# First block of linear attention: loads in longer runs on two queues, plain float32 products, q's maxima on GpSimd

## The chip, the cores and the metric

The kernel runs on one core of one Trainium2 chip. The metric is the device time of one execution in microseconds, the median of several runs.

## The reference

Linear attention over 8 batches, 8 heads, 576 positions and 64 columns, then two feed-forward layers on the 4608 resulting rows of 512:

```python
q_s = exp(q - max(q, axis=-1)); q_s = q_s / (sum(q_s, axis=-1) + 1e-9)
k_s = exp(k - max(k, axis=2));  k_s = k_s / (sum(k_s, axis=2) + 1e-9)
kv  = einsum('bhsd,bhse->bhde', k_s, v)
x   = einsum('bhsd,bhde->bhse', q_s, kv)      # then heads side by side: 4608 x 512
r   = maximum(x @ w_in, 0)                    # 512 -> 2048
x   = (r * r) @ w_out                         # 2048 -> 512
g   = x @ w_gate                              # 512 -> 1536
out = (g / (1 + exp(-g)) * (x @ w_val)) @ w_out2
```

The weights come as 64-bit floating-point numbers; the kernel turns their bits into float32 on chip.

## The kernel before

**Blocks.** The 4608 rows are worked in 9 blocks of 512. For each block the attention of four pairs of heads (hp 0 to 3) gives four tiles xT; the first layer multiplies them by 16 tiles of w_in (`h_mm`, PSUM tiles `ph`), squares the positive part (`g_of`), and multiplies by 16 tiles of w_out into four accumulators (`acc_mm`, tiles `acc`). The main loop interleaves these with the attention of the next block. The gated layer follows for all blocks and is not touched.

**Precision.** Most products are made of float32 values split in two float32r parts, hi (a copy on ScalarE, L104) and lo (the remainder, L105, on VectorE or GpSimd); `mm3` (L110) adds three products of the parts.

**The attention of a pair.** `kv_unit` takes k's maxima over the positions (L336 to L338, a transposition L341, L343, a transposition back L346), subtracts them (L347), takes Exp (L353), and multiplies by v with a column of ones beside it (L358, 12 float32 matmuls of 65 columns, in two halves of the output), so that column 64 holds the sums; L363 and L364 take the reciprocals, L367 scales into `kf`, and `split` writes the parts to `kvs`. `q_unit` takes q's maxima (L376), Exp in 8 activations with the maximum as bias (L380), sums and reciprocals (L383 to L385), and a multiplication on GpSimd (L386). `q_transpose` transposes the result (L393) and splits it; `x_pair` multiplies the parts of kv and qT and splits the product into xT.

**The start.** No work of an earlier block covers the first block. Its tiles lie in slots of the weights' pool `wpb` (`borrowed`). All loads are issued on SP, whose order is the program's (`manual_schedule`): k0 k1 q0 v0 k2 q1 k3 v1 w v2 w q2 q3 w v3, where w is the next raw weight tile. The order on the other engines is a planner's; the program gives each step a tick: `steps` holds for each pair the ticks of kv_unit, q_unit, q_transpose and x_pair, and a unit goes on by one `yield` per tick. Two steps of the weights stand in the same plan, at ticks 5 and 8.

**Weights.** `Weights.step` takes a loaded tile through `bits_of` (L138 on ScalarE, L140, L144 and L148 on VectorE, in a PSUM buffer `pa` that the attention's small products use too; there are two), then a hi copy on ScalarE (L189) and a lo remainder on GpSimd (L191), and loads a further tile. All 32 tiles of the first layer are made while block 0 runs. Later loads reuse buffers that become free when the bits of an earlier tile are done.

## Time and profile before

| | us |
|---|---|
| median of 3 runs | 1699.56 |
| lowest and highest run | 1696.88, 1700.6 |
| the profiled execution | 1697.3 |
| span of its instructions | 1695.2 |
| TensorE busy | 1664.2 (98%) |
| VectorE, ScalarE, GpSimd busy | 930.4, 865.3, 273.8 |
| chain that ended last: TensorE | 91% |

Times in the rows are microseconds from the start of the span, durations of single instructions are nanoseconds where the view says so. PE is TensorE and PEld its weight loads, DVE is VectorE, ACT ScalarE, POOL GpSimd, SP the engine that issues DMAs (SPq: its sequencer). Matmuls overlap, so their busy time is that of the union. `L105` is line 105 of the kernel before, often a helper's line.

### The profile page before, as it was taken

The numbers are of one execution on the slowest core, as the hardware profiler recorded it, in microseconds if no ns is written. First come the engines' busy times: TensorE is split into PE (matmuls) and PEld (weight loads), VectorE is DVE, ScalarE is ACT, GpSimd is POOL, SyncE is SP. The second block draws the span as 40 slices with busy tenths as digits, with TensorE's granted clock in tenths as the row PEclk, the third lists the DMA queues.
The fourth block names the chain that finished last, engine by engine and source line by source line (L and its number), as shares of the span: only waits on it lengthen the run. The fifth ranks groups of instructions, "written<-read, shape, count | busy, mean of one in ns | idle before, by whom it ended". The sixth has DMA issues, their size and how long they took to land.

```text
span 1695.2 us, 23439 instructions
## 1 busy us (share of the span) xinstructions
PE 1664.2 (98%) x8406; PEld 1377.4 (81%) x8406; DVE 930.4 (55%) x1650; ACT 865.3 (51%) x1701; POOL 273.8 (16%) x260
## 2 busy tenths in 40 slices
PE   5999999999999999999999999999999999999998
PEld 3778888878888887788788888888878888888898
DVE  7884545555554564554242457644765476446646
ACT  6885656555565655665443345333543354335434
POOL 2661101112010111111000211021101210121020
PEclk9999999999999999999999999999999999999999
DMA  9653434443443434332233677867686678666897
GB/s 231 177 165 89 128 108 134 144 115 111 128 128 120 144 124 115 108 131 88 81 100 99 191 217 215 248 196 214 212 244 192 205 214 260 197 199 203 252 387 276
DMA packets 221315, 292.00 MB, mean 172 GB/s; under 512 B 124816, under 2 KB 152464, under 8 KB 221200
## 3 DMA queue, kind: packets, MB, share of 16 engines
q1 hardware_dynamic: 220080, 289.33, 55.6%
q8 instruction: 67, 1.10, 0.3%
q10 hardware_dynamic: 1120, 1.18, 0.2%
q14 instruction: 48, 0.39, 0.1%
HBM read 238.55 MB, written 51.90 MB: 171 GB/s over the span
## 4 chain that ended last, share of the span: by engine, by line
PE 91%; DVE 3%; DMA 2%; ACT 2%; issue 1%; POOL 0%; SPq 0%; DVEq 0%; ACTq 0%; POOLq 0%
PE ps L110 45%; PE ph L110 22%; PE acc L110 21%; PE pa L358 1%; PE pa L393 1%; DMA od<-wst 1%; DMA x<-x2d 1%; DVE wst L105 1%; ACT wst L104 0%; ACT w L380 0%; DMA wraw<-in_moe_w_out_dram 0%; DVE wbits L148 0%; DMA kt<-in_k_dram 0%; DVE pa L144 0%; DVE xT L105 0%
## 5 line engine op out<-in xcount | busy, mean ns | idle before, releaser
L110 PE MATMUL ps<-xo,wu 128*128 128x512 f32 (+1 forms) x2520 | 518.2, 368 | 0.0
L110 PEld LDWEIGHTS ps<-xo,wu 128*128 128x128 f32 x2520 | 439.0, 189 | 78.7
L110 PE MATMUL acc<-g,w 128*128 128x512 f32 x1728 | 433.1, 396 | 4.6 <-ACT g L104 1.8
L110 PE MATMUL ph<-xT,w 128*128 128x512 f32 x1728 | 421.4, 393 | 2.3 <-ACT w L189 1.2
L110 PEld LDWEIGHTS ph<-xT,w 128*128 128x128 f32 x1728 | 321.8, 188 | 72.9 <-ACT w L189 1.6
L110 PEld LDWEIGHTS acc<-g,w 128*128 128x128 f32 x1728 | 316.3, 188 | 76.1 <-DVE g L105 4.1
L110 PE MATMUL ps<-uo,wu 128*128 128x512 f32 (+1 forms) x1260 | 259.9, 368 | 1.3 <-DVE uo L105 1.3
L110 PEld LDWEIGHTS ps<-uo,wu 128*128 128x128 f32 x1260 | 219.3, 189 | 41.2 <-DVE uo L105 2.1
L460 ACT ACTIVATE r<-ph 128x512 f32<-128x512 f32 x144 | 86.3, 599 | 220.6 <-PE ph L110 220.2
L105 DVE TENSOR_TENSOR g<-r,g 128x512 fp32r<-128x512 f32 x128 | 91.5, 715 | 190.4 <-ACT g L104 190.4
L104 ACT CAST uo<-u 128x512 fp32r<-128x512 f32 (+1 forms) x210 | 120.8, 580 | 124.7 <-PE ps L110 53.4
L659 POOL TENSOR_TENSOR u<-u 128x512 f32<-128x512 f32 (+1 forms) x30 | 35.4, 1181 | 761.2 <-DVE u L655 761.2
L105 DVE TENSOR_TENSOR uo<-u,uo 128x512 fp32r<-128x512 f32 (+1 forms) x210 | 131.6, 645 | 47.4 <-ACT uo L104 47.3
L654 DVE TENSOR_TENSOR u<-u,ps 128x512 f32<-128x512 f32 (+1 forms) x60 | 38.0, 634 | 215.9 <-ACT u L653 215.9
L609 ACT COPY ps<-ps 128x512 f32<-128x512 f32 x126 | 72.0, 571 | 136.6 <-PE ps L110 135.4
L461 ACT ACTIVATE r<-r 128x512 f32<-128x512 f32 x144 | 91.2, 633 | 3.0
L104 ACT CAST g<-r 128x512 fp32r<-128x512 f32 x144 | 89.4, 621 | 3.2
L235 POOL TENSOR_TENSOR wsum<-wbits 128x256 f32<-128x256 f32 x36 | 35.3, 990 | 308.4 <-DVE wbits L148 255.0
L380 ACT ACTIVATE qs<-qs,qm 128x64 f32<-128x64 f32 x256 | 69.6, 340 | 21.0 <-DVE qm L376 15.5
L386 POOL TENSOR_TENSOR qs<-qs,qr 128x512 f32<-128x512 f32 x32 | 34.4, 1076 | 250.8 <-DVE qr L385 146.5
L653 ACT ACTIVATE u<-ps 128x512 f32<-128x512 f32 (+1 forms) x60 | 33.4, 556 | 51.6 <-PE ps L110 51.5
L618 ACT COPY p<-ps 128x512 f32<-128x512 f32 x63 | 37.1, 588 | 41.6 <-PE ps L110 40.9
(111 smaller groups left out, 1404.5 us busy)
## 6 DMA issues: line engine op xcount, KB each, us to landing
wu<-gvd SPq DMA_DIRECT2D x210, 512.0 KB, 4.4
wu<-od SPq DMA_DIRECT2D x105, 512.0 KB, 4.4
gvd<-wst SPq DMA_DIRECT2D x84, 256.0 KB, 2.3
od<-wst SPq DMA_DIRECT2D x42, 256.0 KB, 2.2
w<-in_moe_w_in_dram SPq DMA_DIRECT2D x16, 512.0 KB, 6.5
w<-in_moe_w_out_dram SPq DMA_DIRECT2D x16, 512.0 KB, 5.2
x2d<-e SPq DMA_DIRECT2D x32, 256.0 KB, 2.4
x<-x2d SPq DMA_DIRECT2D x32, 256.0 KB, 5.4
```

Source lines behind the costliest of these rows:

```text
L104: nc.scalar.copy(hi, src)
L105: (eng or nc.vector).tensor_tensor(lo, src, f32(hi), op=ALU.subtract)
L110: nc.tensor.matmul(ps, lhsT=w[s], rhs=x[t], start=start and n == 0, stop=stop and n == 2, skip_group_check=more,)
L235: nc.gpsimd.tensor_tensor(to, x, y, op=op)
L380: nc.scalar.activation(t[:, j, h], t[:, j, h], AF.Exp, bias=m[:, j, h:h + 1])
L386: nc.gpsimd.tensor_tensor(t, t, r.unsqueeze(3).to_broadcast([P, TJ, 2, D]), op=ALU.mult)
L460: nc.scalar.activation(r, ph, AF.Relu)
L461: nc.scalar.activation(r, r, AF.Square)
L609: nc.scalar.copy(x, y)
L618: nc.scalar.copy(x, y)
L654: nc.vector.tensor_tensor(u, u, gate, op=ALU.mult)
L659: nc.gpsimd.tensor_tensor(s1, a21, a22, op=ALU.add)
```

## The change

- **v** lies in its tile as ones, two rows of 64 columns, ones: 130 columns for two chunks, so each transferred run is 512 B instead of 256 B. Of a pair of chunks the first is multiplied with the ones ahead of it, the second with the ones behind it, and the sums gather in columns 0 and 65 of the product. Column 65 is opened by two matmuls of one column of zeros (`zero`) for every kv_unit; L363 adds both columns.
- **q of block 0** is one DMA per pair, with runs of 1 KB, into a tile in the order (h, j); q_unit writes its result to a second tile in the order (j, h).
- **Queues**: v0 and v1 are issued on ScalarE; SP's order becomes k0 q0 k1 q1 k2 v2 q2 k3 v3 q3 w w w. ScalarE does one Exp of a single column ahead of its loads.
- **Block 0 in plain float32**: every pair has a kf of its own (`first[hp][1]`); q_transpose only copies; x_pair is one float32 matmul of 512 columns. The split of kv into `kvs`, which block 1 needs, moves to tick 10, its remainder to GpSimd.
- **q's maxima**: for pairs 1 to 3 of block 0 GpSimd adds the negative maxima to the whole tile, and ScalarE takes one Exp of 512 columns instead of 8 of 64.

```diff
--- before.py
+++ after.py
@@ -278,7 +278,8 @@
 
     kvs = [att.tile([P, NP, 2, P], F32R, name=f"kv{i}") for i in range(2)]
     kf = att.tile([P, P], F32, name="kf")
-    vt1 = att.tile([CK, 2, NC, D + 1], F32, name="vt")
+    vt1 = att.tile([CK, 2, NC // 2, 2 * D + 2], F32, name="vt")
+    zero = const.tile([P, 1], F32, name="zero")
     kts, qs, qT, xT = {}, {}, {}, {}
 
     def load_k(b, hp, t=None):
@@ -287,12 +288,22 @@
         nc.sync.dma_start(t, k[b, 2 * hp:2 * hp + 2].rearrange("h (p c) d -> p h c d", c=NC))
         return t
 
-    def load_v(b, hp, t=None):
+    def v_words(words):
+
+        t = words[:CK, 0:NC * (2 * D + 2)].rearrange("p (h m e) -> p h m e", h=2, m=NC // 2)
+        v_ones(t)
+        return t
+
+    def v_ones(t):
+        nc.gpsimd.memset(t[:, :, :, 0:2 * D + 2:2 * D + 1], 1.0)
+
+    def load_v(b, hp, t=None, by=nc.sync):
         if t is None:
             t = vt1
         for h in range(2):
-            nc.sync.dma_start(
-                t[:, h, :, 0:D], v[b, 2 * hp + h].rearrange("(p c) d -> p c d", c=NC)
+            by.dma_start(
+                t[:, h, :, 1:2 * D + 1],
+                v[b, 2 * hp + h].rearrange("(p m x) d -> p m (x d)", m=NC // 2, x=2),
             )
         return t
 
...
-    def kv_unit(b, hp):
+    def kv_unit(b, hp, kf=kf):
...
@@ -353,31 +363,51 @@
         pk = ps_a.tile([P, T], F32, name="pa", tag="pa")
+        for j in range(2):
+            nc.tensor.matmul(
+                pk[j * D:(j + 1) * D, D + 1:D + 2], lhsT=kt[:, j, 0, :], rhs=zero[:CK],
+                start=True, stop=False, skip_group_check=True,
+            )
         for c in range(NC):
+            m, x = divmod(c, 2)
             for j in range(2):
                 nc.tensor.matmul(
-                    pk[j * D:(j + 1) * D, 0:D + 1], lhsT=kt[:, j, c, :], rhs=vt[:, j, c, :],
-                    start=(c == 0), stop=(c == NC - 1),
+                    pk[j * D:(j + 1) * D, x:x + D + 1], lhsT=kt[:, j, c, :],
+                    rhs=vt[:, j, m, x * (D + 1):(x + 1) * (D + 1)],
+                    start=(c == 0), stop=(c == NC - 1), skip_group_check=True,
                 )
         rd = col.tile([P, 1], F32, name="rd", tag="rd", bufs=1)
-        nc.vector.tensor_scalar(rd, pk[:, D:D + 1], EPS, None, op0=ALU.add)
+        nc.vector.tensor_scalar(rd, pk[:, 0:1], pk[:, D + 1:D + 2], EPS, op0=ALU.add, op1=ALU.add)
         nc.vector.reciprocal(rd, rd)
         for j in range(2):
             r = slice(j * D, (j + 1) * D)
-            nc.scalar.activation(kf[r, r], pk[r, 0:D], AF.Copy, scale=rd[r])
+            nc.scalar.activation(kf[r, r], pk[r, 1:D + 1], AF.Copy, scale=rd[r])
+        if b:
+            kv_split(b, hp, kf)
+        yield
+
+    def kv_split(b, hp, kf, eng=None):
         kv = kvs[b % 2]
-        split(kv[:, hp, 0], kv[:, hp, 1], kf)
-        yield
+        split(kv[:, hp, 0], kv[:, hp, 1], kf, eng)
 
     def q_unit(i, hp):
 
         t = qs.pop((i, hp))
         m = sp.tile([P, TJ, 2], F32, name="qm", tag="qm")
-        nc.vector.tensor_reduce(m, t, axis=AX.X, op=ALU.max, negate=True)
-        yield
-        for j in range(TJ):
-            for h in range(2):
-                nc.scalar.activation(t[:, j, h], t[:, j, h], AF.Exp, bias=m[:, j, h:h + 1])
+        src = t
+        if i == 0:
+            src, t = src[0].rearrange("p h j d -> p j h d"), t[1]
+        nc.vector.tensor_reduce(m, src, axis=AX.X, op=ALU.max, negate=True)
+        yield
+        if i == 0 and hp:
+            nc.gpsimd.tensor_tensor(
+                t, src, m.unsqueeze(3).to_broadcast([P, TJ, 2, D]), op=ALU.add
+            )
+            nc.scalar.activation(t, t, AF.Exp)
+        else:
+            for j in range(TJ):
+                for h in range(2):
+                    nc.scalar.activation(t[:, j, h], src[:, j, h], AF.Exp, bias=m[:, j, h:h + 1])
         yield
         r = sp.tile([P, TJ, 2], F32, name="qr", tag="qr")
         nc.vector.tensor_reduce(r, t, axis=AX.X, op=ALU.add)
@@ -393,7 +423,9 @@
             nc.tensor.transpose(pt.rearrange("r (p j) -> r j p", j=TJ)[:, j], src[:, j], ident)
         if t is None:
             t = qtp.tile([P, 2, T], F32R, name="qT", tag="qT")
-        split(t[:, 0], t[:, 1], pt)
+            split(t[:, 0], t[:, 1], pt)
+        else:
+            nc.scalar.copy(t, pt)
         qT[i, hp] = t
 
     def x_pair(i, hp):
@@ -402,7 +434,9 @@
         else:
             px = ps_acc.tile([P, T], F32, name="acc", tag="acc")
         t = qT.pop((i, hp))
-        for p0, n, b, _ in runs(i):
+        if i == 0:
+            nc.tensor.matmul(px, lhsT=first[hp][1], rhs=t, start=True, stop=True)
+        for p0, n, b, _ in runs(i) if i else ():
             kv = kvs[b % 2]
             c = slice(p0 * TJ, (p0 + n) * TJ)
             mm3(px[:, c], (kv[:, hp, 0], kv[:, hp, 1]), (t[:, 0, c], t[:, 1, c]), True, True)
@@ -706,20 +740,32 @@
 
 
     with tc.manual_schedule(engines={mybir.EngineType.SP}):
-        nc.gpsimd.memset(vt1[:, :, :, D:D + 1], 1.0)
+        v_ones(vt1)
+        nc.gpsimd.memset(zero, 0.0)
         nc.gpsimd.memset(kf, 0.0)
 
 
         def borrowed():
             return f32(w_slot(wpb)).rearrange("p t n -> p (t n)")
 
+        first = []
         for hp in range(NP):
             kt = borrowed()[:CK, 0:2 * NC * D].rearrange("p (h c d) -> p h c d", h=2, c=NC)
-            vt = borrowed()[:CK, 0:2 * NC * (D + 1)].rearrange("p (h c d) -> p h c d", h=2, c=NC)
-            nc.gpsimd.memset(vt[:, :, :, D:D + 1], 1.0)
-            qt = borrowed()[:, 0:T].rearrange("p (j h d) -> p j h d", h=2, j=TJ)
+            vt = v_words(borrowed())
+            words = borrowed()
+            qt = (
+                words[:, 0:T].rearrange("p (h j d) -> p h j d", h=2, j=TJ),
+                words[:, T:2 * T].rearrange("p (j h d) -> p j h d", h=2, j=TJ),
+            )
             kts[0, hp], qs[0, hp] = (kt, vt), qt
-        for what in "k0 k1 q0 v0 k2 q1 k3 v1 w v2 w q2 q3 w v3".split():
+            words = borrowed()
+            first.append((words[:, 0:T], words[:, T:T + P]))
+            nc.gpsimd.memset(first[hp][1], 0.0)
+        warm = sp.tile([P, TJ, 2], F32, name="qm", tag="qm")
+        nc.scalar.activation(warm[:, 0, 0:1], zero, AF.Exp)
+        load_v(0, 0, kts[0, 0][1], nc.scalar)
+        load_v(0, 1, kts[0, 1][1], nc.scalar)
+        for what in "k0 q0 k1 q1 k2 v2 q2 k3 v3 q3 w w w".split():
             if what == "w":
                 w1.load()
                 continue
@@ -729,15 +775,19 @@
             elif what[0] == "v":
                 load_v(0, hp, kts[0, hp][1])
             else:
-                load_q(0, hp, qs[0, hp])
+                nc.sync.dma_start(
+                    qs[0, hp][0].rearrange("p h j d -> p h (j d)"),
+                    q[0, 2 * hp:2 * hp + 2, 0:T, :].rearrange("h (p j) d -> p h (j d)", j=TJ),
+                )
 
         plan = []
         steps = ((1, 1, 5, 8), (1, 2, 5, 9), (2, 3, 7, 10), (4, 4, 8, 10))
         for hp, (n_kv, n_q, n_t, n_x) in enumerate(steps):
-            plan.append((n_kv, lambda hp=hp: kv_unit(0, hp)))
+            plan.append((n_kv, lambda hp=hp: kv_unit(0, hp, first[hp][1])))
             plan.append((n_q, lambda hp=hp: q_unit(0, hp)))
-            plan.append((n_t, lambda hp=hp: q_transpose(0, hp, w_slot(wpb))))
+            plan.append((n_t, lambda hp=hp: q_transpose(0, hp, first[hp][0])))
             plan.append((n_x, lambda hp=hp: x_pair(0, hp)))
+            plan.append((10, lambda hp=hp: kv_split(0, hp, first[hp][1], nc.gpsimd)))
         plan += [(5, lambda: w1.step(1)), (8, lambda: w1.step(1))]
         tick = run_at(plan)
         for n in range(11):
```

## Rows read from the trace of the kernel before

**Rows 1.** Stretches of 100 us: busy us (and instructions) of each engine, clock, DMA

```profile
0.00:100.00 100.00, 79.60 (x439) 59.16 (x440) 79.20 (x156) 73.14 (x167) 47.98 (x51) 0.97 0.76 201
...
200.00:300.00 100.00, 100.00 (x545) 81.92 (x541) 48.54 (x99) 58.67 (x129) 13.62 (x16) 1.00 0.41 127
...
1000.00:1100.00 100.00, 100.00 (x442) 82.69 (x441) 69.70 (x109) 46.93 (x80) 8.26 (x6) 1.00 0.78 234
```

**Rows 2.** Stretches of 10 us, TensorE alone: busy us, clock, DMA share, GB/s

```profile
20.00:30.00 10.00, 5.86 (x38) 0.73 1.10 308
30.00:40.00 10.00, 7.39 (x45) 0.93 0.74 211
40.00:50.00 10.00, 9.22 (x38) 1.00 0.28 86
```

**Rows 3.** Two chosen stretches: PE, PEld, DVE, ACT, POOL busy, clock, DMA share, GB/s

```profile
4.00:39.57 35.57, 21.61 (x146) 13.81 (x146) 27.88 (x66) 24.16 (x65) 6.41 (x6) 0.90 1.04 250
42.67:100.00 57.33, 55.52 (x284) 43.37 (x283) 48.38 (x87) 46.93 (x99) 37.80 (x31) 1.00 0.63 179
```

**Rows 4.** VectorE's groups, 4.00 to 39.57: busy us, mean ns, idle before, its releasers

```profile
L105 DVE TENSOR_TENSOR w<-pa,w 128x512 fp32r<-128x512 f32 x4 | 2.7, 679 | 0.8 <-ACT w L104 0.8
...
L336 DVE TENSOR_TENSOR m<-w 96x384 f32<-96x384 f32 x4 | 2.2, 552 | 4.1 <-DMA w<-in_k_dram 4.0
L105 DVE TENSOR_TENSOR kv<-kf,kv 128x128 fp32r<-128x128 f32 x4 | 2.1, 533 | 2.9 <-ACT kv L104 2.9
...
L363 DVE TENSOR_SCALAR rd<-pa 128x1 f32<-128x1 f32 x4 | 0.6, 156 | 2.6 <-PE pa L358 1.9 <-ACT kf L367 0.8
```

**Rows 5.** Three chosen stretches of the loads, columns as in group 3

```profile
4.00:6.00 2.00, 0.39 (x1) 0.18 (x1) 1.88 (x6) 0.44 (x1) 0.00 (x0) 1.00 1.21 217
...
24.00:28.00 4.00, 0.99 (x4) 0.70 (x5) 3.34 (x9) 3.96 (x14) 1.51 (x2) 0.58 1.05 381
...
4.00:22.50 18.50, 10.92 (x93) 7.44 (x93) 14.26 (x39) 12.21 (x33) 2.39 (x2) 1.00 1.18 242
```

**Rows 6.** DMA view, 4 to 6 us: packets by size, cumulative

```profile
DMA packets 1714, 0.43 MB, mean 217 GB/s; under 512 B 1708, under 2 KB 1714, under 8 KB 1714
```

**Rows 7.** Instructions in order of time: two loads of v on SP's sequencer

```profile
3.03 1.31 SPq L294 DMA_DIRECT2D w<-in_v_dram  x2
```

**Rows 8.** Groups of ScalarE and GpSimd, 0 to 80 us, columns as in group 4

```profile
L380 ACT ACTIVATE w<-w,qm 128x64 f32<-128x64 f32 x32 | 8.1, 339 | 1.8 <-DVE qm L376 1.8
...
L386 POOL TENSOR_TENSOR w<-w,qr 128x512 f32<-128x512 f32 x4 | 4.5, 1119 | 23.5 <-DVE qr L385 11.1 <-DVE mx L343 10.6 <-DVE rd L364 1.8
...
L104 ACT CAST w<-pa 128x512 fp32r<-128x512 f32 x4 | 2.3, 586 | 0.5 <-PE pa L393 0.5
```

**Rows 9.** Chain that ended last, 80 to 90 us: start, us, what

```profile
81.61 0.85 PE pa L358 x24
...
84.94 0.44 PE pa L393 x4
...
87.45 2.72 PE acc L110 x12
```

**Rows 10.** Instructions in order of time: start, us, what, idle before and releaser

```profile
24.70 0.68 DVE L148 SCALAR_TENSOR_TENSOR wbits<-w,pa 128x512 int32<-128x512 int32 x1
...
25.44 0.45 PE L346 MATMUL pa<-ident,mx 128*96 128x128 f32 x1 [2.57 <-DMA w<-in_moe_w_out_dram]
...
27.53 1.28 POOL L191 TENSOR_TENSOR w<-wbits,w 128x512 fp32r<-128x512 f32 x1
...
27.69 1.27 DVE L105 TENSOR_TENSOR kv<-kf,kv 128x128 fp32r<-128x128 f32 x1 [0.66 <-ACT kv L104]
...
36.97 0.73 PE L110 MATMUL ph<-xT,w 128*128 128x512 f32 x2 [0.23 <-DVE xT L105]
```

**Rows 11.** Line 358: duration ns min/median/max, first and last start

```profile
L358 PE MATMUL pa<-vt,kt x624: 219/222/272, 57.4 to 719.8; 96*64 96x65 f32 x156
```

**Rows 12.** Line 148 in 35 to 135 us, columns as in group 11

```profile
L148 DVE SCALAR_TENSOR_TENSOR wbits<-w,pa x31: 671/679/689, 36.8 to 129.3; 128x512 int32<-128x512 int32 x31
```

More of the change, by code (lines that the diff above doesn't have):

```diff
@@ L306, in load_kv @@
             kt = kt[:CK, 0:2 * NC * D].rearrange("p (h c d) -> p h c d", h=2, c=NC)
-            vt = vt[:CK, 0:2 * NC * (D + 1)].rearrange("p (h c d) -> p h c d", h=2, c=NC)
-            nc.gpsimd.memset(vt[:, :, :, D:D + 1], 1.0)
+            vt = v_words(vt)
         kts[b, hp] = load_k(b, hp, kt), load_v(b, hp, vt)
@@ L714, in borrowed @@
             return f32(w_slot(wpb)).rearrange("p t n -> p (t n)")
+        first = []
         for hp in range(NP):
             kt = borrowed()[:CK, 0:2 * NC * D].rearrange("p (h c d) -> p h c d", h=2, c=NC)
-            vt = borrowed()[:CK, 0:2 * NC * (D + 1)].rearrange("p (h c d) -> p h c d", h=2, c=NC)
-            nc.gpsimd.memset(vt[:, :, :, D:D + 1], 1.0)
-            qt = borrowed()[:, 0:T].rearrange("p (j h d) -> p j h d", h=2, j=TJ)
-            kts[0, hp], qs[0, hp] = (kt, vt), qt
-        for what in "k0 k1 q0 v0 k2 q1 k3 v1 w v2 w q2 q3 w v3".split():
+            vt = v_words(borrowed())
[4 more added lines that the diff above has]
+            )
+            kts[0, hp], qs[0, hp] = (kt, vt), qt
+            words = borrowed()
[6 more added lines that the diff above has]
+        for what in "k0 q0 k1 q1 k2 v2 q2 k3 v3 q3 w w w".split():
             if what == "w":
```

## Prediction

> **What bounds the kernel now.** I read the busy time of TensorE by stretches first. From 200 us on it has work all the time: 100.00 of 100 us, in the later stage too [rows 1]. There only instructions taken from or added to TensorE count. The hole is at the start: 79.60 of the first 100 us [rows 1], and by stretches of 10 from 20 on 5.86, 7.39 and 9.22, part of it at a lower granted clock (0.73 and 0.93 on average, so some of it at 1.2 GHz, the lower of two levels) [rows 2]. So the question is what ends last in the first 43 us, the first block's attention and the first weights.
>
> Next I read VectorE there. From the first landing (4.0) to the end of the bits of the third weight tile (39.57) it is busy 27.88 of 35.57 us, more than ScalarE (24.16) and GpSimd (6.41) [rows 3]. It executes in order, so its 7.69 idle us are waits of whatever stood in front. The groups by operation tell which: 2.9 us before the four kv remainders (hi minus lo, L105), 0.8 before the four qT remainders, 2.6 before L363 [rows 4]. TensorE waits for this chain: the first product h needs all four xT, and these need all four kv and qT.
>
> Last the DMA. In 4.0 to 22.5 us its engines are busy throughout (share 1.18; over 1 because packets overlap) but move only 242 GB/s [rows 5]. Packet size is the likely reason: the stretch 4 to 6, in which all but six of 1714 packets are under 512 B (q and v), moves 217 GB/s, the stretch 24 to 28, mostly weights, 381 [rows 5, 6].
>
> **The change part by part.**
>
> Loads. The first block reads k and v of 8 heads x 576 x 64 and q of 8 x 512 x 64 float32 values, 1.18 + 1.18 + 1.05 = 3.4 MB; v3 now comes after all of it and three weight tiles (1.6 MB). q becomes one DMA of 1 KB runs per pair instead of two of 256 B, v gets 512 B runs, and the weights go behind. With 217 and 381 GB/s as bounds I take 300: 3.4 MB in 11.4 us, so the last attention operand lands near 14 to 15 instead of after 22.5; the first weight follows near 17. Alone this moves nothing in my sum: it keeps VectorE fed, and without it VectorE's idle time would stay. Four v loads are issued by ScalarE; at about 0.65 us each (1.31 us for two on SP [rows 7]) that is 2.6 us of its sequencer, before its first data, while SP has eight fewer issues in the same stretch (15 for 23). ScalarE's early Exp also brings the table load forward; that is worth nothing, since the Exps of q wait for q's maxima (1.8 us, L376 [rows 8]), not for the table.
>
> The Trainium skill, "DMA: Bandwidth & Descriptors", section "Issuing engines are not separate DMA queues", speaks against the second queue: all issuers share the same 16 engines, and only issue time is saved. The share of 1.18 agrees; by it v0 and v1, issued early, even delay k1 and q1 by part of their bytes, and my sum, which gives the second queue nothing, stays as it is.
>
> Plain float32 in the first block. Four qT remainders leave VectorE: 2.7 us busy with 0.8 us of waits before them. Four kv remainders go to GpSimd, in a late step: 2.1 us busy with 2.9 us of waits [rows 4]. Together 8.5 us between 4.0 and 39.57. Only the 4.8 us of work is sure to go; part of the waits may reappear in front of the next instruction. Late next is then the pair of kv sums L363, which waits for TensorE (2.6 us). ScalarE's copies stay. The kv buffers of their own also remove the wait for the shared kf.
>
> x_pair becomes one float32 product of 512 columns. Four float32 transposes of 128 columns take 0.44 us at the full clock [rows 9]; the float32 products of L358 appear as two instructions each (24 for 12), so I take 2 x 0.44 = 0.88 us against three of 2.72/12 = 0.227, 0.68 us [rows 9]. Only the last of the four is on the path: +0.2 us (-0.2 if the remainder pass were hidden in the present rows, +0.9 at the lower clock).
>
> q's maxima on GpSimd. For three pairs 8 activations of a 64-column slice, 8.1/4 = 2.03 us per pair, become one of 512 columns; the nearest row, a copy of 128x512, is 0.59 [rows 8]. ScalarE loses 3 x 1.4 = 4.3 us, GpSimd gains three subtractions of about 1.1 us (its multiplication of the same size: 1.12 [rows 8]). The latency of a pair is 1.1 + 0.6 + a handover, about 1.8 against 2.03: nothing in the sum. ScalarE's 4.3 us lie beside VectorE's work, and would count only if ScalarE ended last.
>
> More GpSimd work has a price on VectorE. A kv remainder that met a GpSimd subtraction (27.53 to 28.81) took 1.27 us and ended with it; the other three account for 2.1 - 1.27 = 0.86, so 0.29 each [rows 4, 10]. That is 0.98 us per meeting. At risk are the twelve maxima operations L336 to L338, which read two SBUF tiles; L347 reads PSUM. None met GpSimd in the start before (L336: 0.55 in all four [rows 4]). I take 1.5 us, between none and one meeting for each of the three new subtractions (3.0).
>
> The Trainium skill, "SBUF — State Buffer", section "SBUF: two separate sides", says the same: VectorE and GpSimd hold a shared port pair exclusively, and the loser waits for the whole instruction. The 1.27 us row agrees; by that rule alone the price would be whole GpSimd instructions, as in the 3.0.
>
> The start then: 8.5 - 1.5 = 7.0 us earlier (4.8 - 3.0 = 1.8 at worst; 8.5 + 2.6 = 11 if L363's waits go too), less 0.2 for the last x.
>
> Zero matmuls. Every kv unit gets two float32 matmuls of one column, with a weight load each: two passes for two column halves, four instructions. In the start they hide; in blocks 1 to 7 there are 7 x 4 = 28 units, and TensorE waits for nothing there. The 24 instructions of a unit take 0.85 us of the chain [rows 9], each about 0.22 from start to end and so overlapped [rows 11], and the halves run side by side, so 12 steps of 0.071. Two more cost 0.14 if a step is set by its weight load, which has 64 columns as all others; if by its streamed columns (1 against 65), near nothing, and I put 0.05 as the issue of four instructions. I take 0.11, nearer the loads: 28 x 0.11 = 3.1 us (1.4 to 4.0). L363 reads a second column in the same instruction: nothing.
>
> The longer runs of v from block 1 on save DMA time that TensorE's 100.00 hides. GpSimd's kv remainders at the end of the start: 4 x about 0.5 (a quarter of 1.28 [rows 10] plus overhead), not needed before block 1.
>
> Sum: -7.0 + 0.2 + 3.1 = -3.7 us. The profiled execution took 1697.3 (span 1695.2 and 2.1 around it), so 1693.6 on its scale; it is 2.3 below the median of the three runs, and on the median's scale the forecast is 1699.56 - 3.7 = 1695.9.
>
> **The rivals.**
>
> The start ends on the weight bits instead. Now the broadcast of kv3's maxima, L346, starts at 25.44, just after L148 of the first weight (24.70 + 0.68): both use the two PSUM buffers named pa, and TensorE idled 2.57 us before it [rows 10]. If the order of the buffers stays, kv3 waits for a weight that now lands later (near 17), with its bits done near 22.5. The chain behind it took 25.44 to 36.97, where the last two products of h start [rows 10]; without the kv split it is about 0.7 shorter. The gain is then 2.9 + 0.7 = 3.6 us, and the time 1699.56 - 3.6 + 3.3 = 1699.3. For it: the weight's step still stands at tick 5, ahead of kv3's at tick 6. Against: the order is planned from due times, and a weight that comes last may be put behind.
>
> The gain is given back in block 0, and the kernel gets slower. TensorE eats a pair of weight tiles in 24 x 0.227 = 5.4 us, and VectorE, ScalarE and GpSimd make them just in time: VectorE is busy 48.38 of 57.33 us from 42.67 to 100 [rows 3], and the last of the 32 tiles has its bits only at 129.3 [rows 12]. If that supply keeps its dates (SP's loads of weights wait for buffers that earlier bits free, so they too are dated by them), an earlier TensorE only waits in between. It decides the sign when more than about 6.6 of the 7 us are lost; with all of it lost and the zero matmuls at 0.14 the time is 1699.56 + 0.2 + 4.0 = 1703.8. Against: bits wait for VectorE, which is freed earlier, so the whole line should move.
>
> That the change doesn't do what it says: TensorE could not be fed earlier because k0 still lands at 4.0. This is no case of its own; it is the lower end of the first rival.
>
> **How the numbers follow.** Forecast 0.48 (1695.9; own range 1691 to 1698.5), first rival 0.37 (1699.3), second 0.15 (1703.8). The range should leave out 2 in 10: the lowest tail of the forecast and most of the second rival, so 1691.0 to 1702.0; that takes in 1.4 to 4.0 for the zero matmuls and a start gain from 1.8 to 10. A measurement can tell about 0.2%, 3.4 us, from no change. Faster by more (below 1696.2) 0.47: the forecast nearly whole, as its small gains, which fall within, weigh about as much as the first rival's large ones; within 0.37; slower 0.16, the second rival and a first rival with dear zero matmuls.
>
> **What would show it.** Right: the last two products of h's first tile start near 30 instead of 36.97; the third weight's L148 ends near 32.5 instead of 39.57; VectorE's L105 in the start has only xT left; L358 rows of block 1 and later have 4 more instructions and take 0.1 us more per unit. First rival: L346 of kv3 again right behind L148 of the first weight. Second rival: TensorE's busy time in 40 to 130 falls by as much as the start gained, and the last L148 stays near 129. The prediction is wrong if one-column matmuls cost nothing, if GpSimd's subtractions lock VectorE many times, or if the planner puts ScalarE's weight conversions ahead of the attention and lets it wait for a weight.

## The result and the profile after

The changed kernel took 1717.34 us (median of 5 runs, 1716.63 to 1718.98) beside 1700.6 (1696.88 to 1703.24) for the kernel before on the same chip: ratio 1.0100, 95% interval 1.0084 to 1.0116. It is slower by 1%, 16.7 us; 1695.9 was forecast, and 1702.0 was the upper end. Its profiled execution has a span of 1715.7 us, 20.5 more than before; the execution profiled before lies 3.3 us below the median of this comparison, the changed one at its own.

TensorE's stretches of 100 us, as in [rows 1] but TensorE alone (busy us, instructions, granted clock, DMA share, GB/s), and below them those of 10 us, as in [rows 2]:

```profile
0.00:100.00 100.00, 77.74 (x444) 0.97 0.67 193
...
1000.00:1100.00 100.00, 100.00 (x436) 1.00 0.76 225
```

```profile
20.00:30.00 10.00, 7.42 (x44) 1.00 1.09 320
30.00:40.00 10.00, 7.42 (x52) 1.00 0.49 152
40.00:50.00 10.00, 8.78 (x25) 0.66 0.41 127
```

The start has not become fuller: 77.74 us of the first 100 where 79.60 were. It has more work in 20 to 30 and less in 40 to 50, at a granted clock of 0.66. The line that nobody would look at is that of 1000 to 1100: TensorE is busy 100.00 us, as before, and the clock is 1.00, but 436 instructions stand where 442 stood [rows 1].

So I followed four dates, the starts of single products, from the trace of each kernel: A, the last (12th) product of h's first tile; B, the first product h of block 1 (the 193rd); C, the first product of the gated layer; and the last product of all. Before they stand at 37.30, 140.55, 912.75 and 1690.49. The table has the differences from these, in us, for all kernels of this study (e1 to e16 are told below), with the medians, each against the kernel before in the same comparison. One execution stands behind each row of dates, and that of the kernel before is a quick one (see above), so most of the dates stand higher than the medians, by up to 5.7 us (e15). Stages without any edit differ by up to 3.7 us (e13 between B and C), in part by the granted clock: in e5, e6, e12, e13, e15 and e16 it stood at its lower level (1.2 GHz) for 3.4 us between 833 and 844, in the kernel before it did not, and the stretch from block 8's first product to C took 1.7 to 2.5 us longer there. TensorE in 830 to 840, before and then e13:

```profile
830.00:840.00 10.00, 9.16 (x40) 1.00 0.47 184
```

```profile
830.00:840.00 10.00, 8.20 (x30) 0.83 0.73 275
```

| kernel | median | ratio (95%) | A | B | C | last |
|---|---|---|---|---|---|---|
| after | 1717.34 | 1.0100 (1.0084 to 1.0116) | +2.2 | +4.2 | +7.4 | +20.3 |
| e1 | 1711.91 | 1.0076 (1.0059 to 1.0093) | +0.6 | +0.6 | -0.1 | +12.0 |
| e2 | 1717.51 | 1.0110 (1.0095 to 1.0125) | +2.1 | +4.2 | +8.3 | +20.0 |
| e3 | 1714.77 | 1.0093 (1.0078 to 1.0109) | +2.9 | +4.2 | +7.0 | +19.4 |
| e4 | 1715.51 | 1.0092 (1.0073 to 1.0111) | +1.5 | +2.0 | +4.9 | +21.0 |
| e5 | 1703.84 | 1.0021 (1.0010 to 1.0033) | +1.0 | +3.1 | +7.6 | +7.7 |
| e6 | 1699.91 | 0.9996 (0.9985 to 1.0008) | -0.1 | +0.7 | +3.2 | +2.2 |
| e7 | 1699.89 | 1.0001 (0.9989 to 1.0013) | -0.9 | -0.2 | +2.5 | +2.1 |
| e8 | 1701.12 | 1.0011 (0.9998 to 1.0024) | +0.9 | +1.0 | +5.2 | +5.0 |
| e9 | 1700.77 | 1.0010 (1.0000 to 1.0021) | -0.7 | +3.6 | +2.2 | +2.4 |
| e10 | 1698.46 | 0.9997 (0.9986 to 1.0008) | +1.0 | +0.3 | -2.0 | -1.5 |
| e11 | 1696.18 | 0.9982 (0.9973 to 0.9991) | +3.8 | +0.8 | -1.1 | -0.8 |
| e12 | 1705.10 | 1.0033 (1.0020 to 1.0046) | +0.8 | +7.5 | +9.5 | +8.5 |
| e13 | 1701.93 | 1.0008 (0.9999 to 1.0017) | +1.1 | +1.1 | +4.8 | +4.7 |
| e14 | 1701.99 | 1.0011 (1.0000 to 1.0021) | +0.6 | +4.5 | +4.5 | +5.2 |
| e15 | 1705.56 | 1.0024 (1.0012 to 1.0036) | +2.1 | +6.7 | +8.7 | +10.8 |
| e16 | 1704.35 | 1.0023 (1.0012 to 1.0033) | +0.7 | +6.1 | +6.2 | +5.9 |

The first row says where the 20.3 us are: 4.2 by the end of block 0, 3.2 in blocks 1 to 7, and 12.8 from C on, in a layer whose code the change does not touch. Of the 4.2, 2.2 stand at A and 2.0 come between A and B. There TensorE waits no longer than before, but it is busy longer, since the granted clock stood at 1.2 GHz from 40.4 to 47.2. TensorE from A to B, before and then after:

```profile
37.30:140.55 103.25, 98.26 (x518) 1.00 0.53 151
```

```profile
39.48:144.74 105.26, 100.65 (x534) 0.97 0.50 148
```

Why the start gained nothing, VectorE's groups in 4 to 40 us show, columns as in [rows 4]:

```profile
L105 DVE TENSOR_TENSOR xT<-acc,xT 128x512 fp32r<-128x512 f32 x4 | 2.8, 690 | 4.0 <-ACT xT L104 4.0
...
L346 DVE TENSOR_TENSOR m<-w 96x384 f32<-96x384 f32 x4 | 2.2, 553 | 7.0 <-DMA w<-in_k_dram 7.0
L140 DVE TENSOR_SCALAR pa<-pa 128x512 int32<-128x512 int32 x3 | 2.1, 700 | 4.7 <-ACT pa L138 4.6
...
L348 DVE TENSOR_TENSOR m<-m,m 96x128 f32<-96x128 f32 x4 | 1.4, 360 | 0.0
```

The waits before kv's remainders (2.9), qT's (0.8) and L363 (2.6) are gone [rows 4], as the prediction had it. In their place stand 4.0 us before xT's remainders, where there were none, 4.7 before L140 (none), and 2.9 more before k's maxima (7.0 for 4.1). In the stretch of [rows 3] VectorE is now busy 22.37 us instead of 27.88: 5.5 us of work went, 5.5 us of waits came. Of the work 4.8 us are the eight remainders; the rest went only from this stretch, since by its end fewer bits of the weights are done.

In the order of time, columns as in [rows 10]:

```profile
24.58 0.63 ACT L138 ACTIVATE pa<-w 128x512 f32<-128x512 f32 x1
25.24 0.70 DVE L140 TENSOR_SCALAR pa<-pa 128x512 int32<-128x512 int32 x1 [2.85 <-ACT pa L138]
...
27.95 0.68 DVE L148 SCALAR_TENSOR_TENSOR wbits<-w,pa 128x512 int32<-128x512 int32 x1
...
28.68 0.31 PE L356 MATMUL pa<-ident,mx 128*96 128x128 f32 x1 [0.32 <-DVE wbits L148]
...
39.15 0.74 PE L110 MATMUL ph<-xT,w 128*128 128x512 f32 x2 [0.81 <-DVE xT L105]
```

The transposition of kv3's maxima (L346 before, L356 now) starts right behind L148 of the first weight, as the first rival wanted it, but at 28.68 where it started at 25.44. The last two products of h's first tile follow at 39.15, before at 36.97 [rows 10].

### The profile page after: what moved, and what is told of

Read it like the earlier page. It is cut to its first block, busy times and chain, and to the rows that moved or that the text cites. A ratio compares the mean times of both kernels' runs of the same rounds, so it can differ in the third digit from the quotient of the medians.

```text
span 1715.7 us, 23619 instructions
## 1 busy us (share of the span) xinstructions
PE 1682.7 (98%) x8530; PEld 1381.1 (80%) x8530; DVE 946.0 (55%) x1642; ACT 861.0 (50%) x1681; POOL 279.6 (16%) x272
## 4 chain that ended last, share of the span: by engine, by line
PE 91%; DVE 3%; DMA 3%; ACT 2%; issue 1%; POOL 0%; SPq 0%; DVEq 0%; POOLq 0%; ACTq 0%
PE ps L110 45%; PE ph L110 22%; PE acc L110 21%; PE pa L374 1%; DMA x<-x2d 1%; PE pa L423 1%; DVE wbits L148 1%; DMA w<-in_v_dram 0%; ACT pa L138 0%; PE pa L367 0%; DMA kt<-in_k_dram 0%; DMA wraw<-in_moe_w_out_dram 0%; DVE pa L144 0%; DMA w<-in_q_dram 0%; ACT w L189 0%
## 5 line engine op out<-in xcount | busy, mean ns | idle before, releaser
L110 PE MATMUL ps<-xo,wu 128*128 128x512 f32 (+1 forms) x2520 | 529.8, 372 | 0.0
L105 DVE TENSOR_TENSOR g<-r,g 128x512 fp32r<-128x512 f32 x128 | 96.6, 754 | 177.8 <-ACT g L104 176.3
```

What stands on the lines that cost most here:

```text
L105: (eng or nc.vector).tensor_tensor(lo, src, f32(hi), op=ALU.subtract)
L110: nc.tensor.matmul(ps, lhsT=w[s], rhs=x[t], start=start and n == 0, stop=stop and n == 2, skip_group_check=more,)
```

## Experiments: the layer that was not touched

**e1 and e2.** The only thing that the change alters for the gated layer is where its tiles lie. `zero`, 128 x 1, takes 32 B of every partition at the beginning of the left of the two sides from which tiles are laid out, and all later tiles of that side move by 32 B; those of the right side stay. e1 adds such a tile to the kernel before and nothing else; e2 makes `zero` of the changed kernel 64 B wide.

```diff
 e1 (on before)
+    pad = const.tile([P, 1], F32, name="pad")
 ...
+        nc.gpsimd.memset(pad, 0.0)
 e2 (on after)
-    zero = const.tile([P, 1], F32, name="zero")
+    zero = const.tile([P, 16], F32, name="zero")[:, 0:1]
```

> The kernel before with one tile more: 128x1 float32 among the constants, set to zero and used by nothing, so that every tile behind it on the same side of SBUF lies 32 bytes further. Placement theory (the gated stage of the changed kernel lost 12.8 us because half of its operands moved by 32 bytes against the other half): matmuls of that stage 4 to 5 ns further apart, time 12 to 13 us over before, about 1712. Rival (the stage is slower for a reason in the changed program's order): time as before, 1700.

> The changed kernel with the constant of zeros 64 bytes wide instead of 4, so that tiles move by 64 bytes instead of 32. Placement theory: the gated stage is as fast as before, time 12 to 13 us under the changed kernel, about 1704.5. Rival (order of the program): 1717, as changed.

e1 alone costs 12.8 us of the median, and 12.9 us between C and the 3000th product behind it. The groups of these products by form in 1000 to 1500 us (duration ns min/median/max, first and last start, of the parts from x), kernel before, after, e1 and e2 in this order:

```profile
L110 PE MATMUL ps<-xo,wu x1444: 389/389/389, 999.8 to 1499.9; 128*128 128x512 f32 x181
```

```profile
L110 PE MATMUL ps<-xo,wu x1402: 388/395/400, 999.7 to 1499.8; 128*128 128x512 f32 x176
```

```profile
L110 PE MATMUL ps<-xo,wu x1406: 388/395/400, 999.6 to 1499.9; 128*128 128x512 f32 x176
```

```profile
L110 PE MATMUL ps<-xo,wu x1406: 387/397/402, 999.7 to 1499.8; 128*128 128x512 f32 x176
```

Before, every one takes 389 ns; with the tiles moved the median is 395 to 397, and 400 to 402 occur. The starts of all the layer's products of 512 columns lie 226.7 ns apart on average before, 231.4 in after and e1, 231.5 in e2.

Divided by the addresses of the operands, the products in after fall into two kinds. Those of the layer's second half (operand `uo`, on the left) keep 227.0 ns where their weights lie on the left too, and take 233.2 where the weights lie on the right. The parts of x lie in two pools, one on each side, and neighbouring products often take theirs from different sides; all of these products are slower, those with one operand on each side most (233.7 to 235.4 ns), but those with both on one side too (231.4 on the left and 230.7 on the right; before, 226.7 and 226.6). So it is not the two operands of one product alone that count; why the others are slowed with them no run shows. The first layer, whose operands all lie on the left, keeps its durations (page's group of g times w: 396 ns in after, in e1 and before). So placement it is; that 64 B would mend it was a wrong guess.

**e5 and e6.** e5 puts `zero` into the attention's pool, which is closed before the gated layer, so that the operands lie as before. e6 asks whether the place itself or the distance counts: on the kernel before it moves both sides by 32 B.

```diff
 e5 (on after)
-    zero = const.tile([P, 1], F32, name="zero")
+    zero = att.tile([P, 1], F32, name="zero")
 e6 (on before)
+    pad = const.tile([P, 1], F32, name="pad")
 ...
-        rd = col.tile([P, 1], F32, name="rd", tag="rd", bufs=1)
+        rd = sp.tile([P, 1], F32, name="rd", tag="rd", bufs=1)
 ...
+        nc.gpsimd.memset(pad, 0.0)
```

> The changed kernel with the constant of zeros on the other side of SBUF, in a pool that is closed before the gated stage, so that all operands of that stage lie where they lay before. Distance theory (32 and 64 bytes both cost the gated stage 12 to 13 us because the two sides of SBUF no longer stand a multiple of 256 bytes apart in their low address bits): gated stage as fast as before, time 1703.5 to 1705. Rival (a second cause in the program's order, since 64 bytes did not help): 1714 or more.

> The kernel before with the unused 32 bytes on the one side as in the first experiment, and one small tile moved out of the pool at the outer end of the other side, so that the operands of the gated stage move by 32 bytes on both sides and keep their distance. Distance theory: gated stage as fast as before, 1699 to 1700.5. Rival (an address that is not a multiple of 64 or 128 bytes is itself slow): as with the 32 bytes alone or slower, 1712 or more.

The same group in e5, and then in e6:

```profile
L110 PE MATMUL ps<-xo,wu x1444: 389/389/389, 999.7 to 1499.9; 128*128 128x512 f32 x181
```

```profile
L110 PE MATMUL ps<-xo,wu x1449: 389/389/389, 999.6 to 1499.9; 128*128 128x512 f32 x182
```

Both are back at 389 and at 226.7 ns between starts. e5's median lies 3.5 us over the kernel before of its comparison, where the changed kernel lay 16.7 over: 13.2 us of it were placement. From C on e5 loses nothing (+7.6, +7.7). e6 takes the time of the kernel before. What counts is the distance between the two sides: by the tiles' addresses, right less left, it is 256 B beyond a multiple of 512 in before, e5 and e6, 224 in after and e1, 192 in e2. The rival, the address itself, fell.

## Experiments: the parts of the start

**e3 and e4**, on e2. e3 issues v0 and v1 on SP behind q1, so that one queue loads all. e4 leaves out the zero matmuls; the first product of a half streams 66 columns instead of 65.

```diff
 e3
-        load_v(0, 0, kts[0, 0][1], nc.scalar)
-        load_v(0, 1, kts[0, 1][1], nc.scalar)
-        for what in "k0 q0 k1 q1 k2 v2 q2 k3 v3 q3 w w w".split():
+        for what in "k0 q0 k1 q1 v0 v1 k2 v2 q2 k3 v3 q3 w w w".split():
 e4
-        for j in range(2):
-            nc.tensor.matmul(... rhs=zero[:CK], start=True, stop=False ...)
```

> As the 64-byte variant, and besides v of pairs 0 and 1 is issued on SP behind q of pair 1, not on ScalarE. Queue theory (SP stood 5.9 us before the load of k2, until the first v load of ScalarE's queue had landed, and with k3 4 us later the whole first block came later): k2 lands before 10 us, the first product of block 0 ends 3 to 5 us earlier than with two queues, time 1700 to 1701.5. Rival (the first weight's bits hold a PSUM buffer that the last pair needs, wherever k3 is): at most 1 us less than the 64-byte variant, 1704.

> As the 64-byte variant without the two matmuls of zeros in each kv unit: the first product has 66 columns instead of 65 and opens column 65 itself, so one value of v is added wrongly to the sums. If a step costs its weight load (0.11 us per unit and more), 28 units give 3 to 4 us back: 1700.7 to 1701.5. If it costs its streamed columns, under 1 us: about 1704.

e3: In the changed kernel SP stood 5.9 us before k2's load, until ScalarE's first v load had landed. The view of waits, SP, 0 to 20 us, of after, and then the longest one in e3:

```profile
SPq L288 <- DMA w<-in_v_dram: 5.9, 1, 5.9
```

```profile
SPq L776 <- DMA w<-in_q_dram: 0.8, 1, 0.8
```

The wait is gone in e3, k2 is issued at 5.37 instead of 8.56, and yet k2 and k3 land at 11.60 and 15.71, within 0.1 us of after (11.65 and 15.78). B is the same, A 0.9 us later than in e2; the median is 2.7 us lower than e2's, with intervals that overlap. Two queues neither cost nor bring anything that can be told here: the bytes take their time in either. The Trainium skill, "DMA: Bandwidth & Descriptors", section "Issuing engines are not separate DMA queues", says that all issuers share the same engines; these dates agree. What delays k2 and k3 (9.65 and 11.67 before) is what newly lies ahead of them: q1 and v1 for k2, v1, v2 and q2 for k3.

e4: from B to the first product of block 6 the run with zero matmuls (e2) lost 3.1 us against before, e4 0.3. Twenty units lie between, so 0.14 us each. e7 and e9 below, on operands that lie well, give 3.2 and 0.3, so 0.15. The rows in after (in order of time, one unit of block 1):

```profile
59.70 0.28 PE L367 MATMUL pa<-zero,kt 96*64 96x1 f32 x4
59.84 0.90 PE L374 MATMUL pa<-vt,kt 96*64 96x65 f32 x24
```

The four start 0.14 us ahead of the unit's products and cost just that: the price of two steps with their weight loads, though one column is streamed. In e4's whole time little of it is seen: from C to the last product e4 lost 16.1 us, e2 11.6. The products of the gated layer take as long in both; but in e4 TensorE waits three times for the remainder of `uo`, and in e2 never. TensorE's waits from 910 on, in e4:

```profile
PE ps L110 <- DVE uo L105: 3.8, 3, 1.5
```

**e7 and e8**, on e5: two ways to keep kv3's maxima from standing behind the first weight in the two buffers `pa`. e7 gives the first block's transposes of q the two idle buffers `ph`; e8 moves the first weights' step from tick 5 to 7.

```diff
 e7, in q_transpose
-        pt = ps_a.tile([P, T], F32, name="pa", tag="pa")
+        if i:
+            pt = ps_a.tile([P, T], F32, name="pa", tag="pa")
+        else:
+            pt = ps_h.tile([P, T], F32, name="ph", tag="ph")
 e8
-        plan += [(5, lambda: w1.step(1)), (8, lambda: w1.step(1))]
+        plan += [(7, lambda: w1.step(1)), (8, lambda: w1.step(1))]
```

> As the variant with the zeros on the other side, and the first block's transposes of q go to the two PSUM buffers of h, which are idle then, instead of the pair pa. Buffer theory (the first block is late because weight bits and the pairs' small products queue for the pair pa): the last two products of h's first tile start 3 to 5 us earlier, time 1700 to 1701.5. Rival (order and landing of the weights alone set it): under 1 us earlier, 1703 to 1704.

> As the variant with the zeros on the other side, and the first step of the weights at tick 7 instead of 5, behind the second transposition of the last pair's maxima. If that transposition behind the bits of the first weight is what holds the last pair: it starts near 22 instead of 28.7, the first tile of h is done 3 us earlier or more, time near 1701. Rival (the bits themselves are what TensorE waits for next, so that later bits cost what the earlier pair gains): within 1 us of that variant.

e7: B 3.2 us earlier than in e5, the median 4.0 us lower. e8: B 2.1 us earlier; the granted clock in 40 to 50 us was 1.00 where e5 has 0.68, and that is where it gains, since A is not earlier. So the times came near what was expected, but not by the way that was given: the buffers date kv3's maxima, and these alone do not date A. Their transposition back (L356, L346 in the kernel before) starts 1.4 us earlier in e8 than in e5 (25.68 for 27.13), and A is the same; in e7 it starts 1.3 us later, and A comes 1.8 earlier; in e12 below it starts 4.5 us earlier than in the kernel before (20.93 for 25.44), and A comes 0.8 later. And the gain is against e5, not against the kernel before: A comes 0.9 us earlier than before in the one, 0.9 later in the other.

**e13 and e14**: one part each on the kernel before. e13 takes q's maxima off on GpSimd, e14 makes the first block's attention plain float32.

```diff
 e13, in q_unit
+        if i == 0 and hp:
+            nc.gpsimd.tensor_tensor(t, t, m...to_broadcast([P, TJ, 2, D]), op=ALU.add)
+            nc.scalar.activation(t, t, AF.Exp)
 ...
 e14
-        split(t[:, 0], t[:, 1], pt)
 ...
+            nc.scalar.copy(t, pt)
 ...
-        for p0, n, b, _ in runs(i):
+        if i == 0:
+            nc.tensor.matmul(px, lhsT=first[hp][1], rhs=t, start=True, stop=True)
 ...
+            plan.append((10, lambda hp=hp: kv_split(0, hp, first[hp][1], nc.gpsimd)))
```

> The kernel before with one part: for three pairs of the first block GpSimd takes q's maxima off (in place), and one Exp of 512 columns follows. Latency theory (the start is a chain of handovers between engines, and this part puts GpSimd's 1.1 us and a handover where eight small Exps stood; ScalarE waited 6.9 us for these subtractions in the changed kernel): last two h products of the first tile 0.3 to 2 us later than 36.97. Rival (ScalarE is relieved by 4 us and the chain gets shorter): 0.5 to 2 us earlier.

> The kernel before with one part: the first block's attention in plain float32 (no remainders of qT, kv's remainders on GpSimd at tick 10), loads and maxima as before. Latency theory (VectorE's busy time was not the bound): VectorE's busy time in 4 to 40 us falls by 4 to 5 us, its idle time there grows by at least 2, and the last two h products of the first tile come at most 2 us earlier than 36.97. Rival (the prediction's step; VectorE's order of work was the bound): they come 4 to 8 us earlier.

e14 is the decisive one. VectorE's busy time in 4 to 40 us, as a chosen stretch, of the kernel before and then of e14:

```profile
4.00:40.00 36.00, 28.31 (x66) 0.91 1.04 252
```

```profile
4.00:40.00 36.00, 23.85 (x58) 0.91 1.04 250
```

4.5 us of work went, and A did not come earlier (+0.6, as in e1, which has no edit of the start); nor did the time fall (1701.99 beside 1700.44). Both kernels have the lower clock for 6.8 us ahead of A. VectorE's groups in e14 show where the 4.5 us went:

```profile
L140 DVE TENSOR_SCALAR pa<-pa 128x512 int32<-128x512 int32 x4 | 2.8, 698 | 5.3 <-ACT pa L138 5.3
...
L387 DVE TENSOR_REDUCE qr<-w 128x8 f32<-128x512 f32 x4 | 2.7, 683 | 2.0 <-ACT w L384 2.0
```

VectorE now waits for ScalarE. L138 of the second weight, on ScalarE, comes at 34.16, and L140 behind it waits 2.04 us. VectorE's order of work was not what ended the start. That the chain of handovers from engine to engine was, which has the same links with fewer instructions on one of them, is read from these waits and not tested by itself. e13 fits it, since it makes one link longer: VectorE waits 4.0 us for the products of kv (1.9 before), ScalarE 2.4 for GpSimd's subtractions, and A to B are 1.1 us later throughout, 0.5 more than in e1. The rivals fell in both.

## Experiments: block 0

**e9, e10 and e11.** e9 is e7 with v as before the change (65 columns, runs of 256 B) and so without zero matmuls. e10 is e9 with the step at tick 7, e11 is e9 with the loads in the order of the kernel before on SP alone.

```diff
 e9 (on e7)
-    vt1 = att.tile([CK, 2, NC // 2, 2 * D + 2], F32, name="vt")
+    vt1 = att.tile([CK, 2, NC, D + 1], F32, name="vt")
 ...
 e10 (on e9)
-        plan += [(5, lambda: w1.step(1)), (8, lambda: w1.step(1))]
+        plan += [(7, lambda: w1.step(1)), (8, lambda: w1.step(1))]
 e11 (on e9)
-        load_v(0, 0, kts[0, 0][1], nc.scalar)
-        load_v(0, 1, kts[0, 1][1], nc.scalar)
-        for what in "k0 q0 k1 q1 k2 v2 q2 k3 v3 q3 w w w".split():
+        for what in "k0 k1 q0 v0 k2 q1 k3 v1 w v2 w q2 q3 w v3".split():
```

> e7 (first block's q transposes in the idle PSUM buffers, zero not in front of the operands) with v as before the change: 65 columns a chunk, runs of 256 B, no zero column and no zero matmuls. Zero-matmul theory (0.14 us for each of the 28 units of blocks 1 to 7, as the run without them gave): first product of block 1 within 1 us of e7's, from there to the gated stage as in the kernel before (within 0.8 us), time 3 to 4 us under e7's, so 1696 to 1697, ratio 0.997 to 0.998. Rival (the start pays back what v's short runs cost there: v lands later, and with it the first block): block 1 starts 1.5 us or more later than e7's, time 1698 to 1700, ratio about 0.999.

> e9 with the first weights' step at tick 7 in place of 5, the two remedies for kv3 together. Both remove the same wait, of kv3's maxima behind the bits of the first weight in the two PSUM buffers pa. If that wait is the only thing, the second adds nothing: time within 1 us of e9. Rival (weight bits date block 0: each tick that they are put back delays block 0's products): first product h later, block 1 starts 0.8 us or more after e9's, time 1 us or more above e9.

> e9 with the loads of the first block in the order of the kernel before, on SyncE alone (k0 k1 q0 v0 k2 q1 k3 v1 weight v2 weight q2 q3 weight v3), q in one DMA a pair. Theory (block 0 is dated by the weights: they land 5 us later when put behind all loads, and their bits hold kv3 and h back): first weight lands near 15 again, first products h at 1 to 2 us before e9's, block 1 starts 0.5 to 2 us earlier, time 1694.5 to 1696. Rival (attention loads decide, as the prediction had it: v3 late again): last two h products of the first tile 1 us or more later than e9's, time 1697 to 1700.

e9: blocks 1 to 7 no longer lose, as expected, but B comes 3.7 us later than in e7, although A differs by 0.2. The gain of one place is lost in another (1.4 us of it in waits of TensorE, 2.1 in longer busy time, see the end of this section). e10 is 2.3 us faster than e9, where nothing or a loss was expected; its A is 1.7 us later and its B 3.3 us earlier. e11 is the fastest of all, 0.18% under the kernel before, with the latest A (+3.8) and its first product h at 36.46 where the kernel before has it at 28.22. The reason that I had given, weights that land earlier (15.2 for 18.2), did not make A earlier, so the time was right and the reason was not shown. But the three together say something: A, on which the prediction's whole start hung, does not decide B.

**e12, e15 and e16.** e12 is the kernel before with the transposes of the first block in `ph` (e7's edit alone). e15 and e16 are e12 and e9 with the first kv unit of block 1 two ticks later.

```diff
 e15 (on e12) and e16 (on e9)
-            for hp, n in enumerate((2, 9, 16, 26)):
+            for hp, n in enumerate((4 if i == 1 else 2, 9, 16, 26)):
```

> The kernel before with one edit: the first block's four q transposes in the two PSUM buffers ph, which are idle there, in place of the two named pa. Buffer theory: the 2.57 us that TensorE idled before kv3's L346 shrink, since pa is no longer shared with the transposes: last two h products of the first tile 1 to 2.5 us earlier than 36.97, time 1697.5 to 1699.5, ratio about 0.999. Rival (in the kernel before VectorE's two passes for each split and the late v3 set the end, the buffers don't): milestones within 0.5 us, ratio 1.000.

> e12 with the first kv unit of block 1 at tick 4 in place of 2. In e12 VectorE stood 2.7 us (1.7 and 1.0) at 51 to 54 us for that unit's transposes, which stand behind full runs of products in TensorE's order, and the weights' bits stood behind it. Theory (that order costs block 0 the 7.5 us): the 14th weight lands 1.5 us or more before e12's 62.8, block 1 starts 3 to 8 us before e12's 148.1, time 1697 to 1702. Rival (the bits are late for another reason, such as the buffers that the weights wait for): block 1 starts within 2 us of e12's, time 1703 to 1706.

> e9 with the same edit. In e9 VectorE stood 3.6 us (2.9 and 0.7) there, and block 1 started 3.6 us after the kernel before's. Theory: block 1 starts 2 to 5 us before e9's 144.1, time 1696 to 1698.5. Rival: within 1 us of e9's, time 1700 to 1701.

e12 starts its second tile of h 0.5 us earlier than the kernel before and ends it 1.3 us earlier, and B comes 7.5 us later. The buffers alone are no gain. What TensorE waited for in 56 to 132 us, of the kernel before (the longest) and then of e12:

```profile
PE acc L110 <- POOL g L105: 1.3, 1, 1.3
```

```profile
PE acc L110 <- POOL g L105: 3.8, 3, 1.4
PE ph L110 <- POOL w L191: 3.5, 3, 1.7
```

It waits for weights and for g. The 14th weight lands at 62.8 in e12 and 62.2 in e9, before at 60.1, and in e7 at 57.2: its load is issued when bits of an earlier tile are done, at 58.2 in e12, and those were late. In front of them VectorE had stood for the first kv unit of block 1, whose transposes lie behind whole runs of products in TensorE's order. VectorE's waits in 38 to 62 us, of e12 and then of e9:

```profile
DVE mx L343 <- PE pa L341: 1.7, 1, 1.7
DVE kt L347 <- PE pa L346: 1.0, 1, 1.0
```

```profile
DVE mx L351 <- PE pa L349: 2.9, 1, 2.9
DVE kt L355 <- PE pa L354: 0.7, 1, 0.7
```

That looked like the cause, but e15 and e16 speak against it: two ticks later VectorE still waits (1.6 us for L346 in e15), B is 0.8 us earlier in the one and 2.5 later in the other. In e15 the 14th weight did land at 58.2, 4.5 us before e12's, as the theory asked, and B followed by only 0.8. The theory fell as stated.

What lies between A and B can be divided by the trace. In the kernel before TensorE is idle there for 5.0 us and busy for 98.3 at the full clock. In e12, e15 and e16 it waits 4.3, 2.7 and 2.7 us longer, in all other kernels between 1.9 less and 0.8 more. The rest is busy time: in the kernels in which the granted clock stood at 1.2 GHz for a stretch behind A (after, e2 to e5, e7, e9, e12, e14 to e16; 3.4 to 6.8 us of it) TensorE is busy 1.3 to 3.4 us longer, in the others not. TensorE from A to B in e14, whose B is 4.5 us late, and then in e12:

```profile
37.87:145.06 107.19, 101.46 (x518) 0.97 0.50 145
```

```profile
38.14:148.08 109.94, 100.65 (x519) 0.98 0.47 140
```

So of e14's 3.9 us between A and B 3.2 are busy time and 0.8 waits. That waits for weights and g date block 0 is shown for e12, e15 and e16 alone; which step of the order makes the supply late there is open, and so is what lets the clock fall in one kernel and not in another.

## Why the prediction was wrong

Two terms failed, the first two below, in the order of their size; the others follow.

- **"Later stages unchanged."** The sum has no term for the gated layer, because no instruction of it changes. It lost 12.8 us by the profile, and e5 puts the placement at 13.2 us of the median. With that term alone at its measured value the forecast would have been 1709. No row of before could have shown its size, but the diff showed a new tile in a pool that lies in front of all others; I read it as a column of zeros and counted its matmuls.
- **Start, -7.0 us.** A came 2.2 us later, B 4.2, in e5 1.0 and 3.1. It was not the clock that held A back: in after it was full up to 40.4, while the kernel before had 1.2 GHz from 24.6 to 31.5. The working took 8.5 us of work and waits off VectorE and let the end of the start move with it, with 1.8 us as the worst case. e14 has 4.5 us less work and no gain: the step that failed is the first reading of the profile, that a VectorE busy 27.88 of 35.57 us bounds the stretch. Its 7.69 idle us already said that it was one link of a chain. "Only the 4.8 us of work is sure to go" holds for the work, not for time: the bound had to reach to zero and beyond. The 2.0 us behind A, at the lower clock, stand in no term. And that the first product h needs all four xT is so only for its first tile as a whole: its first product starts at 28.22 in the kernel before.
- **The first rival** described what happened: L356 of kv3 stands right behind L148 of the first weight, and from it to the last two products of the tile 10.5 us pass, where it reckoned 10.8. Its price was wrong. It set the bits at about 22.5 and they were done at 28.6. Some 2.9 us of that are the landing, at 19.86 where "near 17" was estimated from 300 GB/s; the rest is the way from there, since ScalarE, with the attention ahead in its order, came to L138 only at 24.58 (all loads of the attention had landed at 17.7, not 14 to 15; in 4 to 17.7 us the DMA moved 237 GB/s). "A weight that comes last may be put behind" did not come true.
- **The second rival**, a gain that block 0 gives back, could not show itself in a kernel with no gain, but e12 shows its mechanism, and dearer than it said: TensorE waits 4.3 us longer than before between A and B for weights and g. e9 gives back its 0.7 us and 3.6 more, yet mostly by the clock (3.4 us more of busy time, 0.8 of waits), which is not what the rival said.
- **Zero matmuls, +3.1 (1.4 to 4.0).** Measured 0.14 to 0.15 us a unit, 3.9 to 4.1 us for 28: the bound "set by its weight load", not the value between. Only 24 of the 28 run behind B, 3.4 to 3.5 us; the four of block 1 run in block 0, where TensorE does wait.
- **Contention, +1.5 (0 to 3.0).** The maxima show little: L348 takes 360 ns in the mean where its like L338 took 282, 0.3 us for all four; L346 and L347 are unchanged (553 and 284 ns). The term was too large by 1.2.
- **q's maxima, 0.** Alone they brought no gain: A and B come 1.1 us later (e13; 0.6 in e1, without any edit there). The latency was taken as equal; ScalarE's 2.4 us of waits for GpSimd speak against that.
- **Loads.** That the second queue brings nothing was right (e3), and that earlier operands alone move nothing fits (v3 landed at 17.00, before at 23.56, and A came later), though no run has the loads alone.

In sum: of the 16.7 us of the median 13.2 are placement (medians of after and e5) and about 4 the zero matmuls (dates); the rest, about -0.5 and within the noise of both, is for everything that was to bring 6.8.

## What to carry to other kernels

Where a small constant is added to a tuned kernel, look at which tiles it moves: compare the durations of untouched products before and after, and put the constant where it shifts nothing that matters. An engine that is busy four fifths of a stretch is not yet its bound; only if taking work from it shortens the chain (test with one part alone) may the work be counted as time. And a date in the start is worth nothing until the next stage's supply and the granted clock have been followed to the point where TensorE is full again: here A moved by -0.9 to +3.8 us with hardly a trace in the total.

## What the runs showed of the hardware

In the gated layer, whose operands lie on both sides of SBUF, matmuls of 512 columns took 389 ns and followed each other after 226.7 when the addresses of the two sides differed by 256 B beyond a multiple of 512. When they differed by 224 or 192, matmuls with one operand on each side took 392 to 400 ns in the median, 230 to 235 apart; so did, at 393 to 398 and 231 to 237, those with both on one side whose neighbours used the other; those of a stream on the left alone kept 389 and 227. TensorE shows as busy 100.00 of 100 us before and after, and the granted clock is 1.00: only the count of instructions and their duration tell it. Other distances were not tried.

A stretch at the lower clock shows here in the time of TensorE's work and hardly in its waits: with the granted clock at 1.2 GHz for 6.8 us behind A, TensorE's busy time from A to B was 2.4 us longer in after and 3.2 in e14, while its idle time changed by -0.4 and +0.8.
